# Ten in place of eight weight pairs of the second half's second layer by seven products, with a table of places for the work beside the matmuls

## The chip, the core and the metric

The kernel runs on one core of one Trainium2 chip. TensorE (PE) does the matmuls, VectorE (DVE), ScalarE (ACT) and GpSimd (POOL) the rest, SyncE (SP) issues all DMAs. The metric is the device time of one execution in microseconds (us); less is better.

## The reference

A transformer block of two parallel branches on one layer norm, cut to what matters:

```python
xn = _layernorm(x)                       # x: 2048 x 576
qkv = (xn @ wqkv).reshape(B, S, 3, 32, 18)
idx = pos[:, None] - (jnp.arange(8) * 2)[None, :]   # 8 keys, every second one back
logits = einsum("bhsd,bhswd->bhsw", q, kg) * scale  # masked where idx < 0
o = einsum("bhsw,bhswd->bhsd", softmax(logits), vg)
h = xn @ w1 + b1                         # 576 x 4608
act = h * jnp.tanh(softplus(h))          # Mish
return x + o @ wo + act @ w2             # w2: 4608 x 576
```

All is float32. The attention is local, so its logits and values are elementwise products and short sums, not matmuls; nearly all matmul work is in the two layers of the feed-forward branch.

## The kernel before

**Tiling.** The 2048 tokens are worked in two halves hf of 1024, each half in two blocks b of 512 tokens, a block in four tiles of 128. The 4608 hidden units are 36 groups of 128, taken as 18 pairs q. PE works in a rounded float32 type, so each operand is split into a high and a low part and each product takes three matmuls: high x high, high x low, low x high. ACT makes the high part (a cast), DVE or POOL the low part (a subtraction of the high part from the value).

**First layer.** `m1_part` (L741) computes the 2x2 blocks (two token blocks by the two groups of a pair) with seven products in place of eight, in parts 0 to 5 of 18 to 20 matmuls of 512 columns (lines L683, L689), into four PSUM tiles `h`. `mish` behind them: ACT copies h (L717), DVE adds another h (L728), ACT adds the bias and takes the functions (L729 and following), POOL multiplies (L735).

**Second layer.** In the first half `m2_pair` (L776) multiplies directly: for each pair q four chunks of 24 matmuls of 288 columns. In the second half the pairs q = 1 to 2·OC are taken two at a time as a set e = 0 to OC-1, and their 2x2 blocks (token blocks by column halves of 288) are made by seven products: `p_item(e, k)` (L864) is one product, 24 matmuls (L875), added by DVE into the sum of its own name (L881), or copied there by ACT in the first set. With OC = 4 these are q = 1 to 8. The rest, q = 9 to 17 and 0, go by `m2_cols` (L887), the direct form, 4 chunks of 24 matmuls (L896). A set of two pairs is 168 matmuls by seven products, 192 directly. In the second half the pairs come in the order 1 to 17, 0; names of h, act and po there count places from 0, those of weights pairs, so place 8 works with weights 18 and 19, which are pair 9. The order of products in a set is P7, P4, P1, P5, P2, P6, P3.

**What a set needs.** On the left, for each of its two pairs qq = 0, 1, the raw acts of four blocks, kept in slots of other tiles by `raw_act`, and four sums of them: `u_sum` (L817), then the high part `u_high` on ACT (L823) and the low part `u_low` on DVE or POOL (L829) into a tile `u_e_k_qq`. On the right the sums T1 to T4 of the weights and the blocks B11, B21, B22: they are made in the first half, while each pair's w2 is loaded there anyway, by `t_sum` (L304, DVE and POOL), `t_high` (L310, ACT), `t_low` (L315, DVE), `t_keep` (SP, DRAM kept_T; the blocks to kept_B), and fetched in the second half by `p_fetch` into `pw`, four buffers. For a pair that goes directly, the first half stores its two w2 tiles (kept_w) and the second half fetches them (w).

**Attention** is a Python generator per half, moved on by 73 steps. For each pair of head groups: four steps of logits (POOL product `pr` of two tiles, L542; DVE sum L547, put behind and done at the next step), max, exp and normalisation, four steps of values (POOL product `pv`, L580; DVE sum `og`, L586), a DVE transpose (L606) and a store.

**What sets the order.** `plan` is a list of slots. A slot holds one piece of matmul work and a list of background work; `before(i, fn)` puts work into slot i's list. In each slot the order is: work that the last slot postponed, the background list, the held second part of `mish`, then the matmul piece. The slots of the attention's steps (`cuts`) are computed for the first half by a rate for each stretch, for the second by a list `early` of places in each q. Every engine then executes in exactly the order in which its instructions were written; no engine overtakes itself. Two sets, `behind_adds` and `behind_next`, name slots where an attention sum is put behind other work. The preparation of the sums for QKV's product in the second half starts at slot (0, q=9, place 4), that of the output's weights at (1, q=11, place 3).

Of the kernel before, what the change touches and what calls it, by code (L numbers as in the profile page):

```python
# [30 lines left out]
CU = 2 * DH  # L31
OC = 4
Q1 = [*range(1, NP), 0]
# [6 lines left out]
def block_kernel(ctx: ExitStack, tc: tile.TileContext, x, wq, wo, w1, b1, w2, mask, out):  # L40
# [193 lines left out]
    sums, low = {}, {}  # L234
# [277 lines left out]
    pend, soon, tail = [], [], []  # L512
    behind_adds, behind_next, now = set(), set(), [0]

    def attention(hf):
        kqs = [load_kq(hf, k) for k in range(PU)]
        yield
        behind = [None]

        def flush():  # L520
            if behind[0] is not None:
                if now[0] in behind_next:
                    plan[now[0] + 1][0].append(behind[0])
                elif now[0] in behind_adds:
                    tail.append(behind[0])
                else:
                    behind[0]()
                behind[0] = None

        for pair in range(NQ * UQ // PU):  # L530
            n = f"{hf}_{pair}"
# [3 lines left out]
            for k, (kt, q) in enumerate(kqs):  # L535
                for c in range(2):
                    flush()
                    pr = sb.tile([P, hj, W, CU], F32, tag="pr", bufs=2, name=f"pr_{n}_{k}_{c}")
                    j0 = c * hj
                    hh = hj // 2  # L540
                    for x in range(0, hj, hh):
                        nc.gpsimd.tensor_tensor(  # L542
                            out=pr[:, x:x + hh], in0=q[:, j0 + x:j0 + x + hh, None, :].to_broadcast([P, hh, W, CU]),
                            in1=win(kt, 0, CU, j0 + x, hh), op=ALU.mult)

                    def red(pr=pr, k=k, j0=j0, L=L):
                        nc.vector.tensor_reduce(  # L547
                            L[:, k, j0:j0 + hj].rearrange("p j w h -> p (j w h)"),
                            pr.rearrange("p j w (h d) -> p (j w h) d", h=2), axis=AX, op=ALU.add)
# [4 lines left out]
            flush()  # L554
            if hf == 0:
# [19 lines left out]
            for k, vt in enumerate(vs):  # L575
                for h in range(2):
# [8 lines left out]
                    def red(pr=pr, og=og, c0=k * CU + h * DH, last=(k, h) == (PU - 1, 1), pair=pair):  # L585
                        nc.vector.tensor_reduce(og[:, c0:c0 + DH, :].rearrange("p d j -> p j d"), pr, axis=AX,  # L586
                                                op=ALU.add)
                        if last:
# [3 lines left out]
                            else:  # L592
                                soon.append(turn)
                    behind[0] = red
                    if (hf, pair, k, h) == (0, *(4, 0, 1)):
# [4 lines left out]
            kqs = nxt  # L600
        flush()
        yield
# [92 lines left out]
    def raw_act(q, b, j):  # L695
        if not rslot:
# [469 lines left out]

    def before(i, fn):
        plan[max(i, 0)][1].append(fn)

# [228 lines left out]
    for name, k, d in (("T2", 0, 0), ("T2", 1, 1), ("T3", 0, 2), ("B11", 0, 3), ("B11", 1, 4), ("B21", 0, 5),  # L1398
                       ("B21", 1, 6), ("R2", 0, 7), ("T3", 1, 8), ("R3", 0, 9), ("T1", 0, 10), ("T1", 1, 10),
                       ("T4", 0, 11), ("T4", 1, 11), ("B22", 0, 11), ("B22", 1, 11)):  # L1400
        before(i + d, lambda name=name, k=k: z_fetch(name, k))
    i = spot(0, 9, 4)
    for k in range(2):
        for n, steps in enumerate((
# [4 lines left out]
            for kind, name in steps:  # L1409
                f = dict(l=z_load, s=z_sum, h=z_high, o=z_low, k=z_keep)[kind]  # L1410
                d = 30 + 2 * n + (n >= 14) if k else 2 * n if n < 10 else (19, 20, 22, 23, 25, 26, 27)[n - 10]
                before(i + d, lambda f=f, name=name, k=k: f(name, k))
# [96 lines left out]
    marks = [at["q", 0, 2, 0, 1], at["q", 0, 3, 0, 0], spot(0, 1, 0), spot(0, 2 * OC + 1, 0), at["q", 1, 0, 0, 0],  # L1509
             at["z", 0, 0], spot(1, 0, 0)]  # L1510
# [9 lines left out]
    for n in range(steps - len(last_steps)):  # L1520
# [3 lines left out]
    cuts[0] += last_steps  # L1524
    early = {0: (8,), 1: (0, 2, 4, 6, 8), 2: (0, 4, 7), 3: (0, 3, 6), 4: (0, 4, 7), 5: (0, 3, 7), 6: (1, 4, 7),
             7: (0, 4, 7), 8: (1, 4, 8), 9: (1, 3, 7)}
    for q in range(NP):
# [4 lines left out]
    cuts[1] = cuts[1][:steps]  # L1532
    assert len(cuts[0]) == len(cuts[1]) == steps, (len(cuts[0]), len(cuts[1]), steps)
    for hf in range(NH):
        before(cuts[hf][0] - (4, 14)[hf], lambda hf=hf: (att.__setitem__(hf, attention(hf)), next(att[hf])))
# [26 lines left out]
    for k in range(4):  # L1562
        plan[j + (1, 2, 2, 3)[k]][0].append(lambda k=k: o_split(0, k, True))
    for p_ in range(TJ // 2):
# [58 lines left out]
```

## Time and profile before

| | |
|---|---|
| median of the runs | 1107.06 us (1106.83, 1107.06, 1107.4) |
| the profiled execution | 1106.93 us, of it the span 1105.1 us |
| matmuls | 6550 records |
| DVE busy | 849.1 us |
| POOL busy | 790.8 us |
| ACT busy | 499.1 us |
| bytes moved by DMA | 271.60 MB, mean 246 GB/s |

The span is the time from the first to the last instruction in one profiled execution; the 1.8 us more of its own time lie around it. Busy times are sums over an engine's instructions; consecutive instructions on one engine can overlap a little, so a busy time slightly overstates what the engine is taken up. A matmul's duration is its latency: a block of many tells the spacing. A share of busy time is an average over stages of different kinds.

### The profile page before, as it was taken

How to read it: one execution, taken by the hardware profiler on the slowest of the kernel's cores; microseconds unless marked ns; L12 is line 12 of the kernel's file. 1: busy time of each engine (PE TensorE's matmuls, PEld its weight loads, DVE VectorE, ACT ScalarE, POOL GpSimd, SP SyncE). 2: the span in 40 equal slices, each digit the busy share in tenths (PEclk: the TensorE clock that was granted, in tenths of full speed). 3: DMA queues.
4: the chain of work that ended last, by engine and by line, in shares of the span. 5: the costliest groups of instructions: out<-in, count | busy, mean ns of one | idle time of the engine just before them, and what ended most of it. 6: DMA issues, size and time to landing. Idle time of an engine off the chain costs nothing.

```text
span 1105.1 us, 18208 instructions
## 1 busy us (share of the span) xinstructions
PE 1098.0 (99%) x6550; PEld 1014.0 (92%) x6550; DVE 849.1 (77%) x1367; ACT 499.1 (45%) x917; POOL 790.8 (72%) x639
## 2 busy tenths in 40 slices
PE   8999999999999999999999999999999999999998
PEld 7999899999999999999999888989999999999998
DVE  6368788888889888888656567777886777777786
ACT  5544655544545543646333354434433344343353
POOL 2479777776769688685789568567698976867542
PEclk9999999999999999999999999999999999999999
DMA  6899696868777768676598799656674657776674
GB/s 200 286 311 313 231 335 244 283 234 263 254 269 242 272 225 293 234 265 219 171 316 277 237 348 327 228 192 209 222 225 171 211 196 224 244 293 216 181 232 140
DMA packets 178270, 271.60 MB, mean 246 GB/s; under 512 B 53218, under 2 KB 120068, under 8 KB 178180
## 3 DMA queue, kind: packets, MB, share of 16 engines
q1 hardware_dynamic: 178180, 270.44, 72.1%
q8 instruction: 52, 0.85, 0.3%
q14 instruction: 38, 0.31, 0.1%
HBM read 160.39 MB, written 110.00 MB: 245 GB/s over the span
## 4 chain that ended last, share of the span: by engine, by line
PE 92%; DMA 3%; DVE 2%; ACT 1%; SPq 1%; POOL 1%; issue 1%; DVEq 0%; POOLq 0%
PE h L683 28%; PE po L783 21%; PE po L896 11%; PE pq L351 11%; PE po L875 6%; PE h L689 5%; PE o L1079 5%; PE z L449 3%; DMA accP<-in_x 1%; DMA t<-kept_t 1%; DMA kv<-kv_d 1%; SPq L615 1%; DMA pw<-kept_T 0%; POOL act L735 0%; DMA acc<-in_x 0%
## 5 line engine op out<-in xcount | busy, mean ns | idle before, releaser
L783 PEld LDWEIGHTS po<-w,act 128*128 128x128 f32 x1728 | 236.3, 188 | 5.8 <-POOL act L735 0.4
L783 PE MATMUL po<-w,act 128*128 128x288 f32 x1728 | 240.6, 295 | 0.1
L542 POOL TENSOR_TENSOR pr<-q,kv 128x576 f32<-128x576 f32 x128 | 198.1, 1575 | 8.8 <-DMA q<-q_d 5.6
L735 POOL TENSOR_TENSOR act<-c,act 128x512 fp32r<-128x512 f32 x81 | 107.6, 1328 | 127.5 <-ACT act L734 126.1
L580 POOL TENSOR_TENSOR pv<-L,kv 128x576 f32<-128x576 f32 x128 | 177.9, 1488 | 26.1 <-DVE L L573 21.3
L787 DVE TENSOR_TENSOR acc<-po,acc 128x288 f32<-128x288 f32 x288 | 119.2, 448 | 29.2 <-PE po L783 28.3
L351 PE MATMUL pq<-wq,xt 128*128 128x432 f32 x672 | 136.2, 361 | 1.1 <-ACT xt L81 1.1
L896 PEld LDWEIGHTS po<-w,act 128*128 128x128 f32 x960 | 130.9, 188 | 2.8
L896 PE MATMUL po<-w,act 128*128 128x288 f32 x960 | 132.9, 295 | 0.0
L351 PEld LDWEIGHTS pq<-wq,xt 128*128 128x128 f32 x672 | 125.0, 188 | 7.8 <-ACT xt L81 1.6
L729 ACT ACTIVATE c<-c,b1c 128x512 f32<-128x512 f32 x81 | 58.7, 725 | 137.9 <-DVE c L728 137.6
L683 PE MATMUL h<-xt,t 128*128 128x512 f32 x432 | 110.5, 391 | 0.4 <-DVE rt L728 0.4
L683 PE MATMUL h<-S,t 128*128 128x512 f32 x432 | 110.4, 391 | 0.0
L586 DVE TENSOR_REDUCE og<-pv 128x144 f32<-128x1152 f32 x64 | 85.9, 1345 | 24.0 <-POOL pv L580 23.8
L683 PE MATMUL h<-xt,wa 128*128 128x512 f32 x432 | 103.9, 389 | 0.0
L717 ACT COPY c<-h 128x512 f32<-128x512 f32 x81 | 47.4, 585 | 123.1 <-PE h L689 72.0
L547 DVE TENSOR_REDUCE L<-pr 128x64 f32<-128x1152 f32 x64 | 85.8, 1342 | 21.8 <-POOL pr L542 21.7
L683 PEld LDWEIGHTS h<-xt,wa 128*128 128x128 f32 x432 | 81.0, 188 | 16.6
L875 PEld LDWEIGHTS po<-pw,u 128*128 128x128 f32 x672 | 91.9, 188 | 2.2
L875 PE MATMUL po<-pw,u 128*128 128x288 f32 x672 | 93.4, 294 | 0.0
L683 PEld LDWEIGHTS h<-xt,t 128*128 128x128 f32 x432 | 79.1, 188 | 15.3 <-DVE rt L728 0.9
L899 DVE TENSOR_TENSOR accP<-po,accP 128x288 f32<-128x288 f32 x160 | 68.9, 452 | 30.3 <-PE po L896 29.3
(228 smaller groups left out, 1851.4 us busy)
## 6 DMA issues: line engine op xcount, KB each, us to landing
kv<-kv_d SPq DMA_DIRECT2D x64, 396.0 KB, 5.0
kept_t<-t SPq DMA_DIRECT2D x36, 512.0 KB, 4.9
t<-kept_t SPq DMA_DIRECT2D x36, 512.0 KB, 6.6
rw<-in_w SPq DMA_DIRECT2D x36, 320.0 KB, 4.4
kept_wa<-wa SPq DMA_DIRECT2D x18, 640.0 KB, 4.6
kept_w<-w SPq DMA_DIRECT2D x20, 576.0 KB, 4.0
wa<-kept_wa SPq DMA_DIRECT2D x18, 640.0 KB, 5.3
w<-kept_w SPq DMA_DIRECT2D x20, 576.0 KB, 4.3
```

Source lines behind the costliest of these rows:

```text
L351: nc.tensor.matmul(pq[:, 0:432], XT[:, xi, tok], wt[wi][:, hl, 0:432], start=i == 0, stop=i == len(seq) - 1)
L542: nc.gpsimd.tensor_tensor(out=pr[:, x:x + hh], in0=q[:, j0 + x:j0 + x + hh, None, :].to_broadcast([P, hh, W, CU]), in1=win(kt, 0, CU, j0 + ...
L547: nc.vector.tensor_reduce(L[:, k, j0:j0 + hj].rearrange("p j w h -> p (j w h)"), pr.rearrange("p j w (h d) -> p (j w h) d", h=2), axis=AX, ...
L580: nc.gpsimd.tensor_tensor(out=pr[:, x:x + hj].rearrange("p j d w -> p j w d"), in0=L[:, k, x:x + hj, :, h:h + 1].to_broadcast([P, hj, W, DH]),
L586: nc.vector.tensor_reduce(og[:, c0:c0 + DH, :].rearrange("p d j -> p j d"), pr, axis=AX, op=ALU.add)
L683: nc.tensor.matmul(ph, wt[:, wl, wk * P:(wk + 1) * P], X[:, xs, :], start=first and i == 0, stop=last and i == len(seq) - 1, skip_group_ch ...
L735: nc.gpsimd.tensor_tensor(out=a[:, 1, :], in0=t, in1=a[:, 0, :].bitcast(F32), op=ALU.subtract)
L783: nc.tensor.matmul(po, acts[hf, q, b, j][:, al, tok], done["w2", hf, 2 * q + j][:, wl, c * HC:(c + 1) * HC], start=i == 0, stop=i == 5)
L787: nc.vector.tensor_tensor(out=t, in0=po, in1=t, op=ALU.add)
L875: nc.tensor.matmul(po, units[e, k, qq][:, al, tok], w[:, qq, wl, :], start=i == 0, stop=i == 5)
L896: nc.tensor.matmul(po, acts[hf, q, b, j][:, al, tok], done["w2", hf, 2 * q + j][:, wl, c * HC:(c + 1) * HC], start=i == 0, stop=i == 5)
L899: nc.vector.tensor_tensor(out=t, in0=po, in1=t, op=ALU.add)
```

## The change

OC goes from 4 to 5: pairs 9 and 10 of the second half become a fifth set of seven products, e = 4, and their weights' sums are made and stored in the first half. `m2_cols` keeps q = 11 to 17 and 0.

The places of the background work get tables. `before` counts its calls, and the table MOVED (60 entries) gives for some of them another slot (shifted by up to four) or another list of the slot (the one of the matmul piece, or a position in the list). STEPS lists all slots of the attention's steps in both halves in place of the computed ones; from the eleventh on the second half's are 2 to 20 slots earlier. SUMS names seven attention sums of the second half and the slot each is done in, in place of the two `behind` sets. AHEAD lists 15 slots in which the held part of `mish` goes ahead of the background list. The preparation of QKV's sums begins at (0, q=10, place 6), that of the output's weights at (1, q=13, place 0), with closer steps. The raw acts of (q=10, block 1, group 0) get another slot.

The diff, cut to its core (the tables by a few rows):

```diff
-OC = 4
+OC = 5
+MOVED = {90: (0, 1, 0),
+ 106: (0, 0),
...
+ 749: (0, 0),
...
+STEPS = ((21, 22, 24, 26, 28, 30, 33, 38, 50, 51, 59, 61, 69, 71, 79, 81, 89, 92, 99, 104, 109, 110, 119, 121, 126, 128, 129,
...
+ (260, 261, 262, 263, 264, 267, 269, 273, 276, 279, 280, 283, 285, 288, 292, 295, 298, 299, 302, 304, 307, 311, 315,
...
+SUMS = {(1, 11): (285, 1),
...
+AHEAD = (124, 127, 129, 197, 304, 305, 306, 315, 322, 347, 353, 354, 358, 401, 424)
...
+        def flush(all_=False):
+            for n in list(waiting):
+                if all_ or (hf, n) not in SUMS:
+                    waiting.pop(n)()
...
-                    behind[0] = red
+                    waiting[next(step)] = red
...
-                  (0, 1): (("raw", 3), ("mn", 4), ("mn", 1)), (1, 1): (("tt", 0), ("tt", 1))}[b, j][q % {(1, 0): 4, (1, 1): 2}.get((b, j), 3)]
+                  (0, 1): (("raw", 3), ("mn", 4), ("mn", 1)), (1, 1): (("tt", 0), ("tt", 1))}[b, j][3 if (q, b, j) == (2 * OC, 1, 0) and OC % 2 else q % {(1, 0): 4, (1, 1): 2}.get((b, j), 3)]
...
-    def before(i, fn):
-        plan[max(i, 0)][1].append(fn)
+    count = itertools.count()
+
+    def before(i, fn, how=1):
+        n = next(count)
+        d, h, *place = MOVED.get(n, (0, how))
+        todo = plan[max(i + d, 0)][h]
+        todo.insert(place[0] if place else len(todo), fn)
...
-    i = spot(0, 9, 4)
+    i = spot(0, 2 * OC, 6)
...
-            plan[s2][0 if (e, k, qq) == (0, 6, 1) else 1].append(lambda e=e, k=k, qq=qq: u_sum(e, k, qq))
+            before(s2, lambda e=e, k=k, qq=qq: u_sum(e, k, qq), 0 if (e, k, qq) == (0, 6, 1) else 1)
...
-    behind_adds.update((at["p", "x", OC - 1, 4], at["p", "x", 0, 4], at["s", 1, 2 * OC, 1]))
-    behind_next.add(at["m", 1, 10, 3])
...
+    if STEPS:
+        cuts = [list(c) for c in STEPS]
...
+    for (hf, n), (slot, how) in SUMS.items():
+        plan[slot][how].append(lambda hf=hf, n=n: sums[hf].pop(n, lambda: None)())
...
-    i = spot(1, *(11,3))
+    i = spot(1, 2 * OC + 3, 0)
...
-        k = i + 10 + (2, 5, 10, 15, 20, 25, 30, 35, 40)[n]
+        k = i + 10 + (2, 5, 8, 12, 15, 19, 23, 27, 31)[n]
...
-        for fn in first + bg + (fns + held if i == at["m", 0, 1, 0] else held + fns):
+        for fn in first + (held + bg + fns if i in AHEAD else bg + fns + held if i == at["m", 0, 1, 0] else bg + held + fns):
```

**PE, second half, behind the fourth set.** Names: `po` is a product's or chunk's PSUM tile, `pw_e_k` the right and `u_e_k_qq` the left side of a product, `w2_1_18` and `act_1_1_16` those of the direct form; h1 to h3 belong to the first layer. Before:

```order
L683 MATMUL h1_1_9_9264<-S1_1_6606,t0_1_10_8950 128x512 x6
L896 MATMUL po_1_8_1_0_0_0_9359<-w2_1_18_8900,act_1_1_16_9259 128x288 x3
L896 MATMUL po_1_8_1_0_0_0_9359<-w2_1_19_8925,act_1_1_17_9287 128x288 x3
L896 MATMUL po_1_8_1_0_0_1_9367<-w2_1_18_8900,act_1_1_16_9259 128x288 x3
L896 MATMUL po_1_8_1_0_0_1_9367<-w2_1_19_8925,act_1_1_17_9287 128x288 x3
```

and with the change:

```order
L761 MATMUL h3_1_10_9470<-xt_1_1_6473,t1_1_11_9362 128x512 x6
L953 MATMUL po_4_0_0_0_9484<-pw_4_0_9305,u_4_0_0_9384 128x288 x3
L953 MATMUL po_4_0_0_0_9484<-pw_4_0_9305,u_4_0_1_9460 128x288 x3
L953 MATMUL po_4_0_0_1_9492<-pw_4_0_9305,u_4_0_0_9384 128x288 x3
L953 MATMUL po_4_0_0_1_9492<-pw_4_0_9305,u_4_0_1_9460 128x288 x3
```

Four chunks of 24 for each of the two pairs were there; now seven products of 24 stand for both, the first of them one first-layer pair later.

**DVE, second half, q = 3, around the fifth product (k = 4) of the first set.** `og` and `oT` are the attention's value sums and their transpose, `L` the logits, `u_0_4_1` the low part that PE's product k = 4 reads, `ra0` a raw act of the first layer. Before:

```order
L586 TENSOR_REDUCE og_1_0_7441<-pv_1_0_1_1_7681 128x8x18
L606 STREAM_TRANSPOSE oT_1_0_7770<-og_1_0_7441 128x576
L829 TENSOR_TENSOR u_0_4_1_7743<-rm4_7263,u_0_4_1_7743 128x512
L728 TENSOR_TENSOR ra0_7255<-h2_1_3_7761,ra0_7255 128x512
L829 TENSOR_TENSOR u_0_5_1_7793<-rm3_7262,u_0_5_1_7793 128x512
```

and with the change:

```order
L664 TENSOR_REDUCE og_1_0_7475<-pv_1_0_1_1_7715 128x8x18
L684 STREAM_TRANSPOSE oT_1_0_7804<-og_1_0_7475 128x576
L624 TENSOR_REDUCE L_1_1_7779<-pr_1_1_0_0_7781 128x64
L806 TENSOR_TENSOR ra0_7285<-h2_1_3_7795,ra0_7285 128x512
L907 TENSOR_TENSOR u_0_4_1_7777<-rm4_7293,u_0_4_1_7777 128x512
L907 TENSOR_TENSOR u_0_5_1_7833<-rm3_7292,u_0_5_1_7833 128x512
```

The sum of the logits, which stood behind the product's four adds, now stands ahead of u_0_4_1, and so does the add into ra0.

**POOL at the same place.** `accP3` is a sum of the products, started from the input x. Before:

```order
L861 TENSOR_TENSOR accP3_1_7479<-accP3_1_7479,accP5_1_7477 128x576
L829 TENSOR_TENSOR u_0_4_0_7740<-ra3_7258,u_0_4_0_7740 128x512
L542 TENSOR_TENSOR pr_1_1_0_0_7747<-q_1_2_7447,kv0_1_2_7445 128x576 x2
L829 TENSOR_TENSOR u_0_5_0_7790<-rm2_7261,u_0_5_0_7790 128x512
L817 TENSOR_TENSOR ra3_7258<-ra3_7258,rm2_7261 128x512
L542 TENSOR_TENSOR pr_1_1_0_1_7805<-q_1_2_7447,kv0_1_2_7445 128x576 x2
```

and with the change:

```order
L939 TENSOR_TENSOR accP3_1_7513<-accP3_1_7513,accP5_1_7511 128x576
L907 TENSOR_TENSOR u_0_4_0_7774<-ra3_7288,u_0_4_0_7774 128x512
L619 TENSOR_TENSOR pr_1_1_0_0_7781<-q_1_2_7481,kv0_1_2_7479 128x576 x2
L619 TENSOR_TENSOR pr_1_1_0_1_7809<-q_1_2_7481,kv0_1_2_7479 128x576 x2
L907 TENSOR_TENSOR u_0_5_0_7830<-rm2_7291,u_0_5_0_7830 128x512
L895 TENSOR_TENSOR ra3_7288<-ra3_7288,rm2_7291 128x512
```

The second pair of attention products moved ahead of the low part u_0_5_0 and the sum ra3.

More of the change, by code (lines that the diff above doesn't have):

```diff
@@ L1 @@
+import itertools
 from contextlib import ExitStack
@@ L31 @@
 CU = 2 * DH
-OC = 4
+OC = 5
+MOVED = {90: (0, 1, 0),
+ 106: (0, 0),
+ 107: (0, 0),
+ 111: (0, 1, 0),
+ 152: (-1, 1),
+ 161: (0, 0),
+ 200: (0, 0),
+ 278: (0, 0),
+ 282: (-1, 1),
+ 284: (-1, 1),
+ 286: (-2, 1),
+ 296: (-2, 1),
+ 299: (0, 0),
+ 307: (-2, 1),
+ 308: (-2, 1),
+ 384: (-1, 1),
+ 389: (-1, 1),
+ 407: (0, 0),
+ 442: (1, 1),
+ 537: (0, 0),
+ 546: (2, 1),
+ 547: (2, 1),
+ 549: (0, 0, 0),
+ 557: (0, 1, 0),
+ 558: (1, 1),
+ 573: (2, 1),
+ 610: (-1, 1),
+ 714: (-1, 1),
+ 749: (0, 0),
+ 805: (0, 0),
+ 807: (0, 0),
+ 809: (-2, 1),
+ 812: (0, 0, 0),
+ 817: (0, 0),
+ 821: (0, 0),
+ 831: (0, 0),
+ 840: (0, 0),
+ 850: (-1, 1),
+ 866: (-4, 1),
+ 867: (0, 1, 0),
+ 943: (0, 1, 0),
+ 949: (0, 0),
+ 959: (0, 0),
+ 1049: (0, 1, 0),
+ 1091: (2, 1),
+ 1093: (1, 1),
+ 1097: (2, 1),
+ 1103: (-1, 1),
+ 1129: (0, 0),
+ 1170: (0, 1, 0),
+ 1188: (1, 1),
+ 1220: (0, 1, 0),
+ 1224: (-2, 1),
+ 1258: (0, 0),
+ 1259: (0, 0),
+ 1260: (0, 1, 0),
+ 1264: (0, 0),
+ 1265: (0, 0),
+ 1266: (0, 1, 0),
+ 1277: (0, 1)}
+STEPS = ((21, 22, 24, 26, 28, 30, 33, 38, 50, 51, 59, 61, 69, 71, 79, 81, 89, 92, 99, 104, 109, 110, 119, 121, 126, 128, 129,
[6 rows of a table added]
+SUMS = {(1, 11): (285, 1),
+ (1, 18): (304, 1),
+ (1, 19): (307, 0),
+ (1, 24): (321, 1),
+ (1, 36): (355, 0),
+ (1, 55): (399, 1),
+ (1, 65): (418, 0)}
+AHEAD = (124, 127, 129, 197, 304, 305, 306, 315, 322, 347, 353, 354, 358, 401, 424)
 Q1 = [*range(1, NP), 0]
@@ L512, in block_kernel @@
     pend, soon, tail = [], [], []
-    behind_adds, behind_next, now = set(), set(), [0]
+    sums = {}
+    now = [0]
     def attention(hf):
@@ L517, in attention @@
         yield
[L518 to L528, printed above, removed]
+        waiting, step = {}, itertools.count()
+        def flush(all_=False):
+            for n in list(waiting):
+                if all_ or (hf, n) not in SUMS:
+                    waiting.pop(n)()
+        sums[hf] = waiting
         for pair in range(NQ * UQ // PU):
@@ L553, in attention @@
                     yield
-            flush()
+            flush(True)
+            next(step)
             if hf == 0:
@@ L593, in red @@
                                 soon.append(turn)
-                    behind[0] = red
+                    waiting[next(step)] = red
                     if (hf, pair, k, h) == (0, *(4, 0, 1)):
```

15 lines of the change are left out of this document (8 added, 7 removed), and 5 rows, old and new, of the table STEPS.

## The prediction

> **What bounds the kernel now.** First the page: which engine fills the span, and at which clock.
>
> ```profile
> span 1105.1 us, 18208 instructions
> PE 1098.0 (99%) x6550; PEld 1014.0 (92%) x6550; DVE 849.1 (77%) x1367; ACT 499.1 (45%) x917; POOL 790.8 (72%) x639
> PEclk9999999999999999999999999999999999999999
> PE 92%; DMA 3%; DVE 2%; ACT 1%; SPq 1%; POOL 1%; issue 1%; DVEq 0%; POOLq 0%
> ```
>
> PE is busy for 1098.0 of 1105.1 us at an undisturbed clock, and the chain that ended last runs through PE for 92%. The second view is the list of PE's waits, by what released them:
>
> ```profile
> PE warm L65 <- POOL ident masks.py:199: 1.3, 1, 1.3
> PE pq L351 <- ACT xt L81: 1.1, 2, 0.9
> PE ta L75 <- ACT xn L180: 0.9, 2, 0.5
> PE h L683 <- DVE rt L728: 0.4, 1, 0.4
> ```
>
> (us in total, times, longest.) The first three lie at the start or in code that the diff leaves alone; of the 7.1 us in which PE isn't busy, only the last line, 0.4 us, lies where the change works. So the time is PE's instruction count, with nothing to win from waits: the change pays only by matmuls removed, and loses by waits made. No wait of PE for a DMA is in the list.
>
> **Part 1, the matmuls.** The lines view groups them, the chain shows single blocks:
>
> ```profile
> L896 PE MATMUL po<-w,act 128*128 128x288 f32 x960 | 132.9, 295 | 0.0
> L875 PE MATMUL po<-pw,u 128*128 128x288 f32 x672 | 93.4, 294 | 0.0
> 729.65 3.21 PE po L875 x24
> 823.99 3.18 PE po L896 x24
> 828.99 3.18 PE po L896 x24
> ```
>
> The 295 ns of one is its latency; 132.9 us over 960 is a pitch of 0.138 us in the group, and a block of 24 in the chain takes 3.18 us, 0.1325 each. That is the price of a matmul in a stream. Of q=9 and q=10 the change removes 2 x 96 = 192 matmuls of the direct form (960 becomes 768) and adds one more set of seven products of 24, 168 (672 becomes 840). Both forms have the same tile, 128x288, and the same pitch. Net 24 matmuls fewer: 24 x 0.1325 = **-3.18 us**.
>
> The Trainium skill, "TensorE: Matmul & The Clock Gate", section "Back-to-back issue gap", gives a sustained spacing of about 81 ns at N=128 and 131 ns at N=512, which by interpolation is some 100 ns at 288 (an estimate from that page) and would make the saving 2.4 us. No row here has that spacing (3.18 us for 24), so the measurement decides.
>
> **Part 2, the work that goes with it.** In the second half the sums and the high and low parts of the acts of q=9 and 10, in the first half the sums of their weights:
>
> ```profile
> L829 DVE TENSOR_TENSOR u<-rm,u 128x512 fp32r<-128x512 f32 x12 | 13.5, 1125 | 6.2 <-ACT u L823 6.2
> L817 DVE TENSOR_TENSOR rm<-ra,rm 128x512 f32<-128x512 f32 x6 | 6.9, 1155 | 0.9 <-ACT rm L729 0.9
> L881 DVE TENSOR_TENSOR accP<-po,accP 128x288 f32<-128x288 f32 x100 | 40.4, 446 | 13.8 <-PE po L875 7.9 <-POOL accP L861 3.6 <-DMA accP<-in_x 2.3
> L304 DVE TENSOR_TENSOR twT<-rw,rw 128x288 f32<-128x288 f32 x8 | 9.3, 1157 | 0.0
> L315 DVE TENSOR_TENSOR twT<-twT,twhT 128x576 fp32r<-128x576 f32 x16 | 13.8, 894 | 0.2
> L304 POOL TENSOR_TENSOR twT<-rw,twT 128x288 f32<-128x288 f32 x16 | 15.4, 963 | 1.3
> L304 POOL TENSOR_TENSOR twT<-rw 128x288 f32<-128x288 f32 x8 | 10.4, 1299 | 0.0
> L817 POOL TENSOR_TENSOR ra<-ra,rm 128x512 f32<-128x512 f32 x4 | 6.0, 1493 | 0.1
> L310 ACT CAST twhT<-twT 128x576 fp32r<-128x576 f32 x16 | 10.8, 676 | 16.4 <-POOL twT L304 16.2
> L823 ACT CAST u<-ra 128x512 fp32r<-128x512 f32 x22 | 13.5, 622 | 9.8 <-DVE ra L817 5.1 <-POOL ra L817 2.6 <-PE po L875 2.1
> ```
>
> DVE, second half: 6 more sums x 1.16 + 6 more lows x 1.13 - 4 adds x 0.45 = +11.9 us. DVE, first half: 2 x 1.16 + 4 x 0.89 = +5.9 us. POOL: 8 lows come for 8 that go, 2 sums x 1.49 and 4 x 0.96 + 2 x 1.30 of weights = +9.4 us. ACT: 6 more casts x 0.62 + 4 x 0.68 = +6.4 us. None of it is on PE; what hides it is PE's own work in the same stretch, read quad by quad (a quad is one q):
>
> ```profile
> 307.56:331.64 24.08, 24.08 (x147) 22.10 (x146) 21.15 (x34) 10.90 (x19) 19.24 (x17) 1.00 0.74 254
> 331.64:355.72 24.08, 24.08 (x147) 22.09 (x146) 22.16 (x31) 11.47 (x20) 22.09 (x18) 1.00 0.74 241
> 814.76:842.01 27.25, 27.25 (x173) 25.27 (x172) 16.34 (x31) 8.82 (x15) 26.00 (x20) 1.00 0.52 163
> 842.01:866.10 24.09, 24.09 (x149) 22.09 (x147) 17.79 (x29) 9.15 (x13) 19.77 (x17) 1.00 0.64 232
> ```
>
> (Length, then busy time of PE, PEld, DVE, ACT, POOL, then clock, DMA share, GB/s.) The second half's two quads have DVE at 34.1 of 51.3 us; with 11.9 more it is at 46.0, 90%, still under. The first half's q=9 and 10 are the tight ones: 21.15 + 2.95 = 24.10 and 22.16 + 2.95 = 25.11 of 24.08, if nothing else moved: 0.02 + 1.03 = 1.05 us too much. But the new places of the attention steps shift DVE work between quads, busy times here count the overlap of neighbours twice, and a late weight sum only delays a store that is needed half a program later; what could reach PE is an act behind it. Cost taken: 0, bounds 0 and +1.05.
>
> DMA: 13 more issues on SP. In the first half six stores of kept_B and eight of kept_T, 288 KB each, for four of kept_w, 576 KB; in the second seven fetches of 576 KB for four: 3.4 MB in all on top of
>
> ```profile
> DMA packets 178270, 271.60 MB, mean 246 GB/s; under 512 B 53218, under 2 KB 120068, under 8 KB 178180
> pw<-kept_T SPq DMA_DIRECT2D x16, 576.0 KB, 6.7
> ```
>
> that is 1.3%, in quads whose DMA share is 0.52 to 0.74. A fetch takes 6.7 us from issue to landing, less than the two items (5 us each with the first layer's parts between, as the blocks at 823.99 and 828.99 stand) by which four buffers let it run ahead. Taken as 0; if the cover were gone, one late fetch would cost up to its 6.7 us.
>
> **Part 3, the table.** Most of its entries move work by one or two slots, and a slot here is 1.4 to 3.2 us of PE. I looked for those that put work *ahead of* something PE waits for. One place stands out: second half, q=3, the fifth product (k = 4) of the first set. Before, in time order:
>
> ```profile
> 672.27 1.43 POOL L861 TENSOR_TENSOR accP<-accP,accP 128x576 f32<-128x576 f32 x1 [1.17 <-DMA accP<-in_x]
> 673.65 1.30 POOL L829 TENSOR_TENSOR u<-ra,u 128x512 fp32r<-128x512 f32 x1
> 674.91 2.82 POOL L542 TENSOR_TENSOR pr<-q,kv 128x576 f32<-128x576 f32 x2
> 675.85 0.78 DVE L606 STREAM_TRANSPOSE oT<-og 128x576 f32<-128x576 f32 x1
> 676.55 1.73 DVE L829 TENSOR_TENSOR u<-rm,u 128x512 fp32r<-128x512 f32 x1
> 678.20 0.68 DVE L728 TENSOR_TENSOR ra<-h,ra 128x512 f32<-128x512 f32 x1
> 678.94 3.33 PE L875 MATMUL po<-pw,u 128*128 128x288 f32 x24
> 685.08 1.34 DVE L547 TENSOR_REDUCE L<-pr 128x64 f32<-128x1152 f32 x1
> 686.35 0.68 DVE L829 TENSOR_TENSOR u<-rm,u 128x512 fp32r<-128x512 f32 x1
> 687.68 1.63 PE L683 MATMUL h<-xt,t 128*128 128x512 f32 x6 [0.42 <-DVE rt L728]
> ```
>
> Before, the low u_0_4_1 (676.55) is done 0.66 us ahead of PE's product at 678.94. In the change's order DVE has the reduction of the attention's product pr ahead of it, and then the add L728. On DVE there is a wait for POOL: pr ends at 674.91 + 2.82 = 677.73, the transpose was done at 676.63. By these rows: reduction 677.73 + 1.34 = 679.07, add + 0.68 = 679.75, u_0_4_1 between 0.68 (as at 686.35) and 1.73 (as at 676.55) = 680.43 to 681.48. PE needs the low part in its sixth matmul, 678.94 + 5 x 0.1325 = 679.60. So PE waits 0.83 to 1.88 us. Behind it on DVE stand u_0_5_1, the adds of this product and rt1; since PE is later by as much, the 0.42 us wait at 687.68 goes: net +0.4 to +1.5. The other bound: the 1.17 us that POOL waits for accP's DMA need not come again. Then pr ends at 676.56, the reduction follows the transpose without a wait, and u_0_4_1 is done at 679.33 to 680.38: a wait of 0 to 0.78, and with the old one gone -0.42 to +0.4. Ends -0.42 and +1.5, I take the middle, **+0.5 us**.
>
> The rest of the table I cost at nothing: the new set's items stand between the parts of the first layer at the same distances as the fourth set's before, whose PE rows show no wait, and the attention's steps come earlier, into quads with POOL and DVE time left. What it costs if that cover is gone is rival 1.
>
> **Sum.** Profiled execution 1106.93 (span 1105.1 and 1.8 around it): 1106.93 - 3.18 + 0.5 = 1104.25. The median of the runs, 1107.06, lies 0.13 above; I say **1104.3 us**.
>
> **Rivals.** 0.2% is 2.2 us, about what a measurement of this kernel can tell from no change: faster is below 1104.85, slower above 1109.3.
>
> *Rival 1: DVE gives the gain back.* The q=3 place at its +1.5 and the first half's 1.05 us reach PE: 1106.93 - 3.18 + 2.55 = 1106.3. For it: rows as above, and the same low takes 0.68 or 1.73 us. Against: single DVE delays are absorbed by h tiles of four buffers, and quads with DVE at 22.16 of 24.08 show no wait in PE's list. The Trainium skill, "SBUF — State Buffer", section "Who interferes with whom", says that a DVE instruction with two operands in SBUF shares a port with GpSimd and is held while that one reads. The trace agrees with it: the low with pr running beside it took 1.73 us, the add L728, one operand of which is in PSUM, 0.68 with POOL just as busy. It speaks against this change, which adds such instructions on both engines.
>
> *Rival 2, the other side: POOL's lows come late in the new set.* Eight of its lows stand in POOL's queue among the attention's products,
>
> ```profile
> L542 POOL TENSOR_TENSOR pr<-q,kv 128x576 f32<-128x576 f32 x128 | 198.1, 1575 | 8.8 <-DMA q<-q_d 5.6 <-DVE L L547 3.1
> ```
>
> 1.575 us each. A low that ends up behind one more of them than its slack allows stops PE for up to 1.58 us. It decides from the third such low (2 x 1.58 = 3.16, the whole gain); four give 1106.93 - 3.18 + 6.3 = 1110.05. For it: POOL is at 26.00 of 27.25 us in the quad ahead of these items. Against: q=9 and 10 had eight POOL lows before too, with no wait of PE, and the next quad has POOL at 19.77 of 24.09.
>
> *Rival 3: the matmuls don't shrink the end*, because the attention's last steps or the output's weights come later: 1107. Against it: beside PE's 92% the chain holds 3% of DMA and 2% of DVE, so the end follows PE's count.
>
> **Chances.** Forecast (waits under 1.1 us in all) 0.63; rival 1, 0.22; rival 2, 0.11; rival 3, 0.04. The forecast's own range is 1106.93 - 3.18 - 0.42 = 1103.3 less the runs' spread of 0.5, 1102.8, to 1104.85; to hold 8 in 10 it reaches over rival 1 to 1106.8. A little of rival 1 lies below 1104.85: faster 0.64, the rest of it and rival 3 make same 0.25, slower 0.11.
>
> **What would show it.** PE's groups must read x768 and x840, and PE's busy time fall by about 3.2 to 1094.8. PE's waits should have a new line, a product waiting for DVE u, once, 0 to 1.9 us, near 679, and the line for rt gone or smaller. A line with POOL u would be rival 2; several DVE lines, or c or rt lines between 300 and 360 us, rival 1. The forecast is wrong if PE's waits in the middle of the program add up to more than 1.5 us, or if PE's pitch in the new products isn't 0.13 us.

## The result

| | before | changed kernel |
|---|---|---|
| runs of the first comparison | 1107.09 us median (1106.83 to 1108.06, 6 runs) | 1112.76 us median (1110.71 to 1114.22, 6 runs) |
| ratio | | 1.005, 95% interval 1.0038 to 1.0063 |
| the profiled execution | 1106.93 | 1114.06 |

The change makes the kernel slower by 0.5%, where 0.25% faster was forecast. Measured again later, unedited, it was slower by 0.15% (1108.37 us, the last experiment). The spread is as telling as the median: the kernel before stays within 1.3 us here (within 2.6 us over the 29 runs of a later comparison), this one scatters over 3.5 us, and over 6.5 us later. What follows is read from the one profiled execution of 1114.06 us.

The page of the changed kernel, its size, the busy times and the chain:

```profile
span 1112.3 us, 18222 instructions
...
PE 1098.5 (99%) x6526; PEld 1013.1 (91%) x6526; DVE 866.7 (78%) x1381; ACT 503.7 (45%) x927; POOL 799.9 (72%) x647
...
PE 90%; DMA 3%; DVE 3%; POOL 2%; issue 1%; ACT 1%; SPq 0%; POOLq 0%; DVEq 0%; ACTq 0%
...
L953 PE MATMUL po<-pw,u 128*128 128x288 f32 x840 | 118.6, 297 | 2.2 <-DVE u L907 2.2
...
L974 PE MATMUL po<-w,act 128*128 128x288 f32 x768 | 108.0, 297 | 2.8 <-DVE accP L977 2.7
```

The matmuls are as announced, 24 fewer, yet PE is busy for 0.5 us longer and the span has grown by 7.2 us. Both groups now have an idle time ahead of them, in the last column. PE's waits (total, times, longest):

```profile
PE po L974 <- DVE accP L977: 2.7, 1, 2.7
PE po L953 <- DVE u L907: 2.2, 1, 2.2
...
PE po L861 <- DVE acc L865: 0.9, 1, 0.9
...
PE h L761 <- DVE rt L806: 0.3, 1, 0.3
...
PE h L761 <- DVE c L806: 0.2, 1, 0.2
```

6.3 us in the middle of the program where there were 0.4: +5.9. (Measured as the distance of two matmul starts less the usual one, the two long waits are 2.90 and 2.40 us.) The start of the program (the same code) had 0.6 us more of waits in this execution, PE's busy time 0.5 more: 7.0 of the 7.2 us. That PE was busy longer with fewer matmuls is the second half of the story. Two windows of 12 us around the two long waits (length, then busy time of PE, PEld, DVE, ACT, POOL, then clock, DMA share, GB/s):

```profile
678.00:690.00 12.00, 9.76 (x51) 8.81 (x50) 9.20 (x11) 3.77 (x7) 9.85 (x7) 0.86 0.64 195
887.00:899.00 12.00, 9.27 (x45) 8.17 (x44) 9.29 (x13) 6.22 (x8) 7.86 (x7) 0.86 0.12 30
```

The granted clock is 0.86 on average in both, 1.00 in the windows of the other stages. In single matmuls: from 683.76 us on 12 of them start 0.23 to 0.24 us apart instead of 0.132, and one of the first layer takes 0.43 instead of 0.23; from 892.27 us on 13 start 0.24 us apart. So PE runs at about half its pace for some 3 us behind each long wait; this is called half clock below. That costs 0.107 us a matmul, 1.5 and 1.4 us. No such window is in the trace of before, where PE never waited this long.

**The first place, 680 us**, is the one that the prediction named. In order of time:

```profile
673.90 1.43 POOL L939 TENSOR_TENSOR accP<-accP,accP 128x576 f32<-128x576 f32 x1 [1.45 <-DMA accP<-in_x]
...
676.55 5.56 POOL L619 TENSOR_TENSOR pr<-q,kv 128x576 f32<-128x576 f32 x4
...
677.48 0.78 DVE L684 STREAM_TRANSPOSE oT<-og 128x576 f32<-128x576 f32 x1
...
679.41 1.35 DVE L624 TENSOR_REDUCE L<-pr 128x64 f32<-128x1152 f32 x1 [1.15 <-POOL pr L619]
...
679.66 0.82 PE L953 MATMUL po<-pw,u 128*128 128x288 f32 x5
...
680.68 0.68 DVE L806 TENSOR_TENSOR ra<-h,ra 128x512 f32<-128x512 f32 x1
...
681.27 1.40 DVE L907 TENSOR_TENSOR u<-rm,u 128x512 fp32r<-128x512 f32 x1
...
682.72 4.11 PE L953 MATMUL po<-pw,u 128*128 128x288 f32 x19 [2.24 <-DVE u L907]
```

Five matmuls run, the sixth waits for u_0_4_1, which stands behind the logits' sum (1.15 us of wait for POOL and 1.35 of work) and the add into ra0. POOL's product is late because of the input's DMA ahead of it: 1.45 us of wait at 672.45, where it was 1.17 at 671.1 before. With it POOL starts its addition 1.63 us later than before (673.90, 672.27), PE its product only 0.72 us later (679.66, 678.94).

**The second place, 889 us**, was not foreseen. DVE, POOL and PE:

```profile
883.79 2.82 POOL L962 TENSOR_TENSOR accP<-accP,accP 128x576 f32<-128x576 f32 x2
...
885.25 0.42 DVE L639 TENSOR_REDUCE m<-L 128x32 f32<-128x256 f32 x1
885.70 5.18 DVE L641 TENSOR_TENSOR L<-L,m 128x256 f32<-128x256 f32 x1
886.57 1.29 POOL L813 TENSOR_TENSOR act<-c,act 128x512 fp32r<-128x512 f32 x1
...
887.81 2.78 POOL L962 TENSOR_TENSOR accP<-accP,accP 128x576 f32<-128x576 f32 x2
...
890.80 0.68 DVE L806 TENSOR_TENSOR c<-h,c 128x512 f32<-128x512 f32 x1
891.40 1.54 DVE L977 TENSOR_TENSOR accP<-po,accP 128x288 f32<-128x288 f32 x4
...
891.90 1.54 PE L974 MATMUL po<-w,act 128*128 128x288 f32 x5 [2.73 <-DVE accP L977]
```

The subtraction of the maximum, two operands in SBUF, takes 0.42 to 0.43 us in 12 of its 16 executions, and 5.18 here. It ends 0.28 us after POOL has run out of work, at 890.59: POOL has done four instructions in a row, and the subtraction came between none of them. Behind it the adds that empty PSUM are late, and PE waits for a free `po` tile. POOL's additions of product sums (L962) stand behind the last set: with a fifth one they run from 862 to 911 us, where they ran from 812 to 862, and so they meet this subtraction. The trace of before already had one such case, with another of the 16 subtractions, and I had not read it:

```profile
845.58 3.67 DVE L563 TENSOR_TENSOR L<-L,m 128x256 f32<-128x256 f32 x1
```

There PE had matmuls enough in between, and nothing followed from it.

### The profile page after: what moved, and what is told of

The parts are those of the page before. It is cut to its first block, busy times and chain, and to the rows that moved or that the text cites. A ratio compares the mean times of both kernels' runs of the same rounds, so it can differ in the third digit from the quotient of the medians.

```text
span 1112.3 us, 18222 instructions
## 1 busy us (share of the span) xinstructions
PE 1098.5 (99%) x6526; PEld 1013.1 (91%) x6526; DVE 866.7 (78%) x1381; ACT 503.7 (45%) x927; POOL 799.9 (72%) x647
## 4 chain that ended last, share of the span: by engine, by line
PE 90%; DMA 3%; DVE 3%; POOL 2%; issue 1%; ACT 1%; SPq 0%; POOLq 0%; DVEq 0%; ACTq 0%
PE h L761 28%; PE po L861 20%; PE pq L431 11%; PE po L953 8%; PE po L974 8%; PE h L767 5%; PE o L1157 5%; PE z L529 3%; DMA pw<-kept_T 2%; POOL pr L619 1%; DMA q<-q_d 1%; DMA kept_wa<-wa 1%; POOL act L813 1%; POOL accP L962 1%; DVE L L641 0%
## 5 line engine op out<-in xcount | busy, mean ns | idle before, releaser
L861 PEld LDWEIGHTS po<-w,act 128*128 128x128 f32 x1728 | 236.3, 188 | 7.0 <-DVE acc L865 1.3
L861 PE MATMUL po<-w,act 128*128 128x288 f32 x1728 | 240.7, 295 | 1.1 <-DVE acc L865 0.9
L619 POOL TENSOR_TENSOR pr<-q,kv 128x576 f32<-128x576 f32 x128 | 194.3, 1543 | 10.7 <-DMA q<-q_d 6.2
L813 POOL TENSOR_TENSOR act<-c,act 128x512 fp32r<-128x512 f32 x75 | 102.7, 1370 | 117.8 <-ACT act L812 103.6
L865 DVE TENSOR_TENSOR acc<-po,acc 128x288 f32<-128x288 f32 x288 | 117.4, 448 | 23.1 <-PE po L861 22.0
L953 PEld LDWEIGHTS po<-pw,u 128*128 128x128 f32 x840 | 116.2, 190 | 5.4 <-DVE u L907 2.5
L953 PE MATMUL po<-pw,u 128*128 128x288 f32 x840 | 118.6, 297 | 2.2 <-DVE u L907 2.2
L807 ACT ACTIVATE c<-c,b1c 128x512 f32<-128x512 f32 x75 | 54.3, 724 | 137.7 <-DVE c L806 137.5
L974 PEld LDWEIGHTS po<-w,act 128*128 128x128 f32 x768 | 106.0, 190 | 5.9 <-DVE accP L977 3.9
L974 PE MATMUL po<-w,act 128*128 128x288 f32 x768 | 108.0, 297 | 2.8 <-DVE accP L977 2.7
L795 ACT COPY c<-h 128x512 f32<-128x512 f32 x75 | 44.0, 586 | 110.1 <-PE h L767 61.2
L761 PEld LDWEIGHTS h<-S,t 128*128 128x128 f32 x432 | 78.2, 189 | 13.3 <-ACT rm L795 0.5
```

Of the source, the lines that this page charges most:

```text
L619: nc.gpsimd.tensor_tensor(out=pr[:, x:x + hh], in0=q[:, j0 + x:j0 + x + hh, None, :].to_broadcast([P, hh, W, CU]), in1=win(kt, 0, CU, j0 + ...
L761: nc.tensor.matmul(ph, wt[:, wl, wk * P:(wk + 1) * P], X[:, xs, :], start=first and i == 0, stop=last and i == len(seq) - 1, skip_group_ch ...
L813: nc.gpsimd.tensor_tensor(out=a[:, 1, :], in0=t, in1=a[:, 0, :].bitcast(F32), op=ALU.subtract)
L861: nc.tensor.matmul(po, acts[hf, q, b, j][:, al, tok], done["w2", hf, 2 * q + j][:, wl, c * HC:(c + 1) * HC], start=i == 0, stop=i == 5)
L865: nc.vector.tensor_tensor(out=t, in0=po, in1=t, op=ALU.add)
L953: nc.tensor.matmul(po, units[e, k, qq][:, al, tok], w[:, qq, wl, :], start=i == 0, stop=i == 5)
```

## The experiments

The runs were made in three groups, each on one chip and beside the kernel before: the first four below (before: 1107.21 us); the first of the waits made on purpose, the sums back, and POOL back (1106.98); the second run of waits, more places, and the change once more (1106.82). The forecasts start from the change's 1112.8 us, which was measured in none of these groups; its repetition in the third gave 1108.37.

**One table entry less.**

```diff
- 749: (0, 0),
```

> The changed kernel with one table entry less: the low part u_0_4_1 stands on DVE ahead of the logits' sum again, as before the change; nothing else moves. Theory A (the order on DVE is the cause of the wait at 680 us): the product's wait of 2.24 us for u goes, and with it the 16 matmuls at half clock behind it (16 x 0.107 = 1.7 us): 1112.8 - 4.1 = about 1108.7. Rival (POOL's four attention products in a row, 676.55 to 682.11 us, hold the shared port, so the low would not be done before them in any order): the wait stays at 2 us or more and the time at 1112.8.

1108.07 us (1106.46 to 1113.71, 12 runs), ratio 1.002 (1.0006 to 1.0035). In its profile the wait for u is gone; what has come instead:

```profile
PE h L761 <- DVE rt L806: 1.5, 2, 1.2
...
PE h L761 <- ACT ra_r L795: 0.3, 1, 0.3
```

The median is near what theory A forecast, but by luck: the change itself, unedited, later gave the same (1108.37 us, ratio 1.0015), so the time shows no gain of this edit. The trace shows that the wait for u goes with the order, and that the next instructions wait instead. The logits' sum still stands ahead of the add into ra0. ACT executes in order and had waited 5.07 us for that add (3.67 before), so the casts of u_5 and u_6 behind it came late, and rt in the end. And there is a second piece of luck: in this profile the subtraction at 884 us had the same POOL instructions beside it and was let in after the first of them:

```profile
883.88 1.17 DVE L641 TENSOR_TENSOR L<-L,m 128x256 f32<-128x256 f32 x1
```

The twelve times fall into two groups: seven from 1106.46 to 1108.55, all with a mean clock of 1.0, and five from 1111.51 to 1113.71 at 0.997 to 0.998. The means differ by 5.3 us; the hold in the trace above is worth 2.9 + 1.4 = 4.3. That the upper group is the hold is argued from this, since only a run of the lower group was profiled.

**Four additions on POOL later.**

```diff
- 1277: (0, 1)}
+ 1277: (0, 1), 970: (4, 1), 971: (4, 1), 977: (4, 1), 978: (4, 1)}
```

> The changed kernel with four of POOL's additions of product sums (P4 and P5 with P7) four slots later; DVE's order is untouched. Theory B (DVE's subtraction L641 took 5.18 us because POOL ran without a gap; 0.43 is its usual time): it takes under 2 us, PE's wait of 2.73 us for accP at 889 us falls below 0.8 and the half clock behind it (13 x 0.107 = 1.4 us) goes: 1112.8 - 3.6 = about 1109.2. Rival (DVE has too much work there): L641 becomes short, but the wait stays above 2 us and the time within 1 us of 1112.8.

1107.16 us (1105.66 to 1111.02, 11 runs), ratio 1.0002 (0.9993 to 1.001). In the trace theory B holds. DVE's order is the same, the subtraction takes 0.42 us (a row of the timeline):

```profile
882.80 0.42 DVE L641 TENSOR_TENSOR L<-L,m 128x256 f32<-128x256 f32 x1
```

In all five profiles of kernels with this edit (this one and the four below that keep it) it takes 0.42 us; in the four without it, beside POOL's row, 5.18, 1.17, 1.19 and 1.18. The wait for accP at 889 us is gone from PE's list; but it is also missing in the three others without the edit, so its absence in one profile, and the time, prove less. Four of the eleven runs still lie at 1108.35 to 1111.02 with a mean clock of 0.998; none of them was profiled. The wait at 680 us is still there, and this time with no half clock behind it; the list's line, and the window from 677 us:

```profile
PE po L953 <- DVE u L907: 2.2, 1, 2.2
```

```profile
677.00:689.00 12.00, 9.81 (x63) 8.98 (x63) 10.38 (x13) 4.12 (x8) 11.37 (x8) 1.00 0.80 246
```

The clock is 1.00 there, where the changed kernel's profile had 0.86.

**Both, and one low part of the first half.**

```diff
- 749: (0, 0),
- 1277: (0, 1)}
+ 1277: (0, 1), 970: (4, 1), 971: (4, 1), 977: (4, 1), 978: (4, 1), 593: (0, 0)}
```

> Both edits, and one low part of QKV's weight sums behind the four adds ahead of which it stood at 369 us in the first half (a wait of 1.08 us). If the three places carry the loss, and the matmuls removed are worth 3.2 us: 1112.8 - 4.1 - 3.6 - 1.1 = about 1104.0, faster than before by 3 us. Rival (the fifth set's work itself makes DVE late, and a wait removed comes back at the next place): above 1107.

1106.93 us (1106.13 to 1108.42, 11 runs), ratio 0.9998: at the rival's edge, 2.9 us above the forecast. The two groups of times are gone, but in the profile (of the longest run, 1108.42) waits removed came back next door: 0.99 us for c at 373 instead of 1.08 at 369, and 1.15 and 1.35 us for ra_r and rt at 683 and 689 instead of 2.40 for u.

**The fifth set without the tables.**

```diff
-MOVED = {90: (0, 1, 0),
...
+MOVED = {}
+STEPS = ()
+SUMS = {}
+AHEAD = ()
```

> The fifth set alone: all four tables empty, the attention's steps computed as before, work where the general rules put it. If the fifth set's own work is what makes PE wait, this is slow with waits in the quads of the fifth set (850 to 890 us) and in the first half's q = 9 and 10: 1112 or more. If the tables brought the waits in, 1104 to 1106. I expect 1112 to 1116, with waits at other places than the tables' three.

1123.36 us (1120.98 to 1125.17, 4 runs), ratio 1.0145. PE's longest waits:

```profile
PE h L690 <- DVE c L735: 4.9, 3, 2.4
PE h L690 <- DVE rt L735: 4.5, 3, 1.7
PE po L882 <- ACT rm L736: 2.6, 1, 2.6
```

By the general rules the work does not fit between the matmuls: waits from 325 us on, of which those in the first half's q = 9 and 10 and at 874 us, 2.52, 1.94 and 2.77 us, lie where the fifth set adds work. The tables win some 11 of the 16 us back. The forecast of 1112 to 1116 was too kind. These general rules are not those of the kernel before: the list `early`, one mark of the rates and the `behind` sets differ too, so the run doesn't price the fifth set alone.

It settles one thing about the second place. The same subtraction (the 13th of the 16) meets the same row of POOL instructions here, so it does not take the four tables to bring them together:

```profile
896.70 2.82 POOL L891 TENSOR_TENSOR accP<-accP,accP 128x576 f32<-128x576 f32 x2
...
898.62 1.18 DVE L570 TENSOR_TENSOR L<-L,m 128x256 f32<-128x256 f32 x1
...
899.46 1.50 POOL L742 TENSOR_TENSOR act<-c,act 128x512 fp32r<-128x512 f32 x1
...
900.92 2.81 POOL L891 TENSOR_TENSOR accP<-accP,accP 128x576 f32<-128x576 f32 x2
```

It was let in after the first of them and took 1.18 us.

**Waits made on purpose.** In the kernel before, with pairs of an add and a subtraction that cancel, ahead of one add of the first half:

```diff
+                for n in range({2: 14, 5: 16, 8: 18, 11: 20, 14: 22}.get(q, 0) if (b, jj, c) == (1, 2, 0) else 0):
+                    nc.vector.tensor_tensor(out=t, in0=t if n % 2 else po, in1=po if n % 2 else t, op=ALU.subtract if n % 2 else ALU.add)
```

> The kernel before, with 14, 16, 18, 20 and 22 further adds and subtractions of a PSUM tile on DVE ahead of one add of the first half's second layer, at q = 2, 5, 8, 11, 14; the pairs cancel. Each is about 0.385 us (1.54 for four in a row), PE has some 4 us of cover there: waits of about 1.4, 2.2, 2.9, 3.7, 4.5 us. Theory C (a wait of PE over some 2 us may cost half the clock for about 3 us, not every time, and one of 3 us or more does every time): half-clock matmuls behind the two or three longest, some chance at 2.2, none at 1.4. Rival (the half clock at 684 and 892 us in the changed kernel had another cause): no half clock behind any.

The waits came out longer than meant, 4.8, 5.6, 6.6, 7.3 and 9.1 us: each operation took 0.49 us instead of 0.385, and PE had some 2 us of cover instead of 4. Half clock stood behind all five (1151.42 us, one run). The rival falls: the half clock is made by the wait. So a second run with fewer operations (6 to 12):

> As the run of waits by size, with 6, 8, 10, 12, 6, 8, 10, 12 further operations at q = 2, 4, 6, 8, 10, 12, 14, 16: by that run's slope of 0.4 to 0.5 us for one, waits of about 1.5, 2.4, 3.2, 4.0 us, each twice. Theory C (half clock behind a wait by chance between about 2 and 4 us, always above): none at 1.5, some of the middle four, both at 4.0. Rival (a fixed threshold): both of one size behave alike, and none below it has half clock.

1135.82 us, one run; one of the eight places shows no wait over 0.6 us. Four of its waits, by windows of 12 us from just ahead of each; they are 3.15, 3.67, 2.33 and 3.17 us:

```profile
276.00:288.00 12.00, 9.02 (x48) 8.16 (x46) 11.23 (x24) 3.02 (x5) 4.12 (x5) 0.86 0.47 156
329.00:341.00 12.00, 8.49 (x37) 7.67 (x37) 9.08 (x22) 2.45 (x4) 4.51 (x5) 0.72 0.31 97
432.00:444.00 12.00, 9.83 (x56) 9.08 (x55) 10.24 (x20) 3.42 (x6) 4.73 (x4) 0.86 0.89 300
484.00:496.00 12.00, 9.00 (x60) 8.25 (x59) 11.32 (x23) 3.62 (x6) 6.22 (x5) 1.00 0.73 258
```

3.15 us is followed by half clock and 3.17 us, with the same number of operations, is not, which speaks for theory C and against a fixed threshold. With the waits past the first 20 us of all the profiles here (each the distance of two matmul starts less the usual one):

| wait, us | half clock behind it |
|---|---|
| 0.8 to 1.9, nineteen waits | none |
| 1.94, 2.33, 2.40, 2.90, 3.15 | yes |
| 2.35, 2.52, 2.67, 2.77, 3.17 | no |
| 3.67, 4.82, 5.03, 5.62, 6.61, 7.33, 9.06 | yes, all |

**The sums back behind the adds**, on the kernel with the four additions later:

```diff
-SUMS = {(1, 11): (285, 1),
+SUMS = {(1, 9): (282, 0), (1, 10): (285, 1), (1, 11): (286, 0),
```

> The kernel with the joins four slots later (1107.16), and three sums of the logits on DVE at q = 3 put back behind the product's adds, where they stood before the change; POOL's four attention products stay in one row. Theory A2 (the sum ahead of the add into ra0 holds up DVE, and ACT behind it, and so first u_0_4_1, then ra_r and rt): PE's waits between 675 and 692 us, 2.35 us in the kernel with the joins later, fall to 0.8 or less: 1107.2 - 1.7 = about 1105.5. Rival (POOL's four products in a row are the cause): 1.5 us or more remain, about 1107.

1105.18 us (1104.71 to 1107.53, 11 runs), ratio 0.9986 (0.9977 to 0.9995): theory A2's time. Its profile is of one of the two longest runs (1107.49 us; nine lie at 1105.96 or below). In it no wait for u is left at 680 us, though POOL's four products stand as before. A wait for rt of 1.1 us remains, more than the 0.8 of the forecast and less than the rival's 1.5, and one of 0.7 at 665 us for a sum that waits for the input's DMA:

```profile
PE h L761 <- DVE rt L806: 1.4, 2, 1.1
...
PE po L953 <- DVE accP L959: 0.7, 1, 0.7
```

Over the profiles of the change and of the edits that keep its tables, the order decides the wait for u at this place: it is 2.2 to 2.5 us in the three with the logits' sum ahead of u_0_4_1 (the change, its repetition, four additions later), and none in the five in which the sum stands behind it.

**And POOL back as well.**

```diff
- (260, 261, 262, 263, 264, 267, 269, 273, 276, 279, 280, 283, 285, 288, 292, 295, 298, 299, 302, 304, 307, 311, 315,
+ (260, 261, 262, 263, 264, 267, 269, 273, 276, 279, 282, 283, 285, 288, 292, 295, 298, 299, 302, 304, 307, 311, 315,
- 749: (0, 0),
```

> As the kernel with the sums back, and POOL's second pair of attention products behind u_0_5_0 and the sum ra3, u_0_4_1 ahead of ra0: at this place both engines have the order of before the change. By theory A2 the same time as the sums alone within 0.5 us, 1105.0 to 1105.5; by the rival 1.5 us or more below that kernel. What is left of the 3.2 us of removed matmuls is then about 2: 1107.2 - 3.2 + 0.5 (rt wait at 734) + 0.5 (waits at 1000) = 1105.0.

1106.63 us (1105.63 to 1107.96, 11 runs), ratio 0.9997. The rival falls, POOL's order of the change is no loss; but theory A2's time, at most 0.5 us from the sums alone, is missed too: with the old order it is 1.4 us slower. Why, is not settled: its waits in the profile (1.5 us for rt, 0.2 for u) are no longer than those.

**More places.** On the kernel with the sums back:

```diff
- 1277: (0, 1), 970: (4, 1), 971: (4, 1), 977: (4, 1), 978: (4, 1)}
+ 1277: (0, 1), 970: (4, 1), 971: (4, 1), 977: (4, 1), 978: (4, 1), 593: (2, 0), 1252: (0, 0)}
-AHEAD = (124, 127, 129, 197, 304, 305, 306, 315, 322, 347, 353, 354, 358, 401, 424)
+AHEAD = (124, 127, 129, 197, 284, 304, 305, 306, 315, 322, 347, 353, 354, 358, 401, 424)
```

> The kernel with the sums back (1105.2), and three more places in the table: the add into rt ahead of the low part u_6_1 at q = 3 (its wait of 1.1 us at 689 falls to 0.4), the low part of QKV's weight sum one chunk later (0.7 at 369 goes), and one low part of the output's weights behind a chunk's adds (0.2 at 1000 goes): 1105.2 - 1.6 = about 1103.6. Rival (waits move on to the next instruction, as the first rt wait did): above 1104.8.

1104.62 us (1104.15 to 1105.8, 11 runs) beside 1106.82: ratio 0.9982 (0.9973 to 0.999). That lies between the forecast of 1103.6 and the rival's 1104.8. It is faster than the kernel before (by 0.2%) and than the change (1108.37 us beside it). The page's busy times, and what PE still waits for after the start:

```profile
PE 1095.3 (99%) x6526; PEld 1011.0 (92%) x6526; DVE 859.7 (78%) x1381; ACT 503.8 (46%) x927; POOL 799.1 (72%) x647
```

```profile
PE h L761 <- DVE c L806: 0.4, 1, 0.4
PE h L761 <- DVE rt L806: 0.3, 1, 0.3
PE po L953 <- DVE u L907: 0.2, 1, 0.2
```

**The changed kernel once more**, with nothing edited:

> The changed kernel once more, beside the others on one chip: 1112 to 1113. Theory B2 (whether DVE's subtraction L641 is held for four POOL instructions or for one is settled anew in each execution, and with it the wait at 889 us): times in two groups some 4 to 5 us apart, the upper at 1112 to 1114. Rival (the hold follows from the order alone): one group, and the subtraction over 4 us in this profile too.

1108.37 us (1105.51 to 1112.01, 12 runs), ratio 1.0015 (1.0004 to 1.0026). The forecast of 1112 to 1113 is missed, and the rival falls: in this profile the subtraction took 1.19 us with the same order, and there is no wait at 889 us; the one for u at 680 us is there, without half clock:

```profile
PE po L953 <- DVE u L907: 2.5, 1, 2.5
```

```profile
883.78 1.19 DVE L641 TENSOR_TENSOR L<-L,m 128x256 f32<-128x256 f32 x1
```

But theory B2's two clear groups are not there either: the times lie all over the 6.5 us, with clocks from 0.997 to 1.0. With two waits that can each have half clock behind them or not, and one of them there or not, that is no surprise, but which run had what can't be told from the times. Over both comparisons the change's 18 runs have a median of 1110.25 us. Why all six runs of the first comparison lie above 1110 us and only three of the twelve here stays open.

## Why the prediction was wrong

The profiled execution lies 9.8 us above the forecast of 1104.3. By its rows 2.9 of them are half clock, 2.7 the wait at 889 us, 1.3 the place at q = 3 beyond the 0.5 taken, 0.9 the wait in the first half, 0.5 smaller waits and 0.6 the start of the program; part 1 gave some 0.5 less than taken.

- *Part 1, the matmuls, -3.18 us.* Right in count, a little too large. PE's two groups are x768 and x840. In the kernel with more places they take 106.2 and 117.4 us, together 2.7 less than before, and its PE is busy for 1095.3 us, 2.7 below 1098.0. With the waits all but gone the time is 2.2 us below before, 0.3 from the forecast's 1104.3.
- *Part 2, DVE's and POOL's work hidden.* As a sum, yes: in the profile of the change DVE is busy for 17.6 us more than before (17.8 by the forecast), POOL for 9.1 (9.4). The quads of the fifth set show only a wait of 0.14 us at 861 that is its own; the one at 889 is below. The bound of +1.05 in the first half was used up in one profile: 0.9 us for acc at 369 us, in q = 11, not 9 or 10.
- *Part 3, the place at q = 3, +0.5, bounds -0.42 and +1.5.* The right place and the right chain, mis-sized, and the first step that failed: 2.24 us of wait, +1.8 with the old wait of 0.42 gone. The rows gave pr's end at 1.21 us ahead of PE's product; it was 0.29, because POOL got the input's DMA later. I took it from the old trace as a fixed moment and leaned to the side on which it would come earlier. In the profile of the repetition (1107.47 us) it is PE's only wait over 0.4 us past the start, 2.51, and there is no half clock: of the 3.2 us above the forecast 1.6 are this term's.
- *"The rest of the table I cost at nothing."* This is the second step that failed, and the larger one in the profile of 1114.06 us. Its ground was that the new set's items stand at the same distances as the fourth set's before, whose PE rows show no wait. But the fifth set puts POOL's additions of product sums some 50 us later, beside a subtraction of the attention with less cover behind it, and the wait was 2.73 us. The set does this without the tables too, as the run without them shows. I had looked for work put ahead of a piece that PE waits for on the same engine; here the order on DVE was harmless, and a neighbour on another engine held it. In how many of the other runs it did is not known.
- *A wait was priced at its own length.* This step failed too: nowhere did I count what comes behind a wait. Two waits of 2.4 and 2.9 us cost 1.5 and 1.4 us more at half clock. No wait in the trace before was long enough to show that.
- *Rival 1* named the mechanism, DVE held by POOL, and had it at 1106.3; its terms, the q = 3 place and the first half, were 3.1 us of 6.3. *Rival 2*, POOL's lows late in the new set, didn't occur: no wait for POOL u is in any profile. What I said of the two-operand low, that POOL's reading delays it by a microsecond, holds for nearly all: in the trace of before, 152 instructions of DVE with two operands in SBUF took over 0.3 us more than the shortest of their line, and each of them ends at most 0.7 us behind the end of a POOL instruction beside it: 148 behind the first such end, three behind the second, and one, the subtraction, behind the third. The row that I set against it was no contrast: while the add L728 ran at 678.20 us, POOL was idle (from 677.73 to 680.22). Yet of all 778 with an operand in PSUM none took over 0.14 us more than the shortest of its kind. The subtraction is the exception: it was let in at none of two boundaries between POOL instructions in the trace of before, and at none of three in that of the change.

## What to carry to other kernels

Where one engine sets the time and its waits are nil, work removed from it pays only as much as the others can be fitted around, and the cost of a new wait is not its length: above some 2 us it brought 1 to 2.5 us of half clock with it here, by chance up to 3.2 us and always from 3.7 us on. Before moving a step to another slot, look at what runs beside it on an engine that can hold it (here POOL held DVE), not only at what stands behind it in its own queue, and look in the old trace for the same instruction's longest execution, not its mean. A kernel whose times scatter where it did not scatter before may have a race between engines in it, and one profile shows only one outcome of it: before crediting an edit with a gain, measure the unedited kernel beside it.

## What the hardware showed unexpectedly

A subtraction of 0.42 us took 5.18 us beside four POOL instructions in a row, and 1.17 and 1.19 us in two other executions with the same instructions in the same order. The other case, in the order of before, took 3.67 us in all three of its profiles (that of before and the two with waits made on purpose). The Trainium skill, "SBUF — State Buffer", section "Who interferes with whom", calls the port that both engines use an exclusive lock; the traces agree, with the addition that whether DVE gets it between two POOL instructions isn't fixed.

The half clock set in behind waits from 1.94 us on, sometimes, and behind those of 3.67 us and more always; it lasted 2.4 to 5.5 us. The Trainium skill, "TensorE: Matmul & The Clock Gate", section "HAM oscillation — how this bites in real kernels", warns of idle gaps of TensorE over about 3.4 us. That every wait above 3.6 us had it agrees; that five of the ten between 1.94 and 3.17 us had it too says that a gap below 3.4 us is not a safe one here.
